# Attention features of a fused kernel: plain f32 in two row tiles, with a new order of steps

## The chip, the cores and the metric

The kernel runs on one core of a Trainium2 chip. The metric is the device time of one execution in microseconds (us); the median of three runs is given. A profile of one further execution shows every instruction of the core's engines: TensorE (PE in the rows, PEld for its weight loads), VectorE (DVE), ScalarE (ACT), GpSimd (POOL), and the queue that issues DMAs (SP).

## The reference

Three stages follow one another. All arrays are float32.

```python
# attention: q, k, v are (2, 8, 576, 64), omega is (128, 64)
def phi(x):                                   # x is q or k, times 64 ** -0.25
    h = x @ omega.T - sum(x * x) / 2          # 128 features of each row
    return exp(h - max(h)) / sqrt(128)
kv, z = phi(k).T @ v, sum(phi(k), rows)
x = (phi(q) @ kv) / (phi(q) @ z + 1e-6)       # -> 1152 tokens x 512
# first MoE block: w_in (512, 2048), w_out (2048, 512)
h = x @ w_in
x = (h * clip(h + 3, 0, 6) / 6) @ w_out
# second one: 8 experts, each token goes to its best one, at most 288 rows per expert
out[i] = gate[i] * relu(x[i] @ w1[e]) @ w2[e]
```

The weights w_in and w_out come as float64. The kernel leaves out `sum(x * x) / 2`, which is the same for all 128 features of a row and cancels against the maximum.

## The kernel before

**Units.** The attention stage works on 18 units, each one load of 256 KB: 128 partitions by four blocks of 128 columns. A block holds two heads' rows on top of each other (64 partitions each), so that a unit has eight groups of 128 rows. Units 0 to 3 are k of the first batch, unit 4 the remainder of k, then q and k alternate, then the rest of q (13 to 17). `seq` lists them. Omega is laid out as a block matrix, 128 partitions by 2 x 128 columns, one omega in the upper half of the rows for the first 128 columns and one in the lower half for the others.

**Steps of a unit**, each with a letter and the unit's number in the plan:

- XH, XL (`halve_x`): x is rounded to float32r on ScalarE (L786), and the rest is subtracted on GpSimd, for units 0 and 1 on VectorE (L788). Omega is split in the same way (L757, L759).
- B (`features`): for each half of the unit six float32r products, three for each of two blocks (L798), into one PSUM bank.
- N: the negative maximum of each row group on VectorE (L804). P: four exponentials of 128 columns on ScalarE, with that maximum as bias (L810).
- for k: K (`kv_acc`), 16 float32 products in two column tiles, 32 records in the trace (L825), accumulated in the pair of banks called acc; KR for the remainder (L836); KW, KV for the sums.
- for q: C (four transposes, L855), T (copy on ScalarE, L859), D (16 products in two column tiles, L871), R, S, X (division on VectorE, L881 to L893), E (four transposes, L899), EH and EL (the result in float32r halves, L922 and L925).

**What comes behind.** H(f, g) is the hidden product of 128 columns of w_in with a third of the tokens, 12 float32r products of 384 columns (L289); 16 x 3 of them follow. The float64 weights are decoded by integer work, mostly on VectorE (L258 to L268), then split (L274, L276; the first four subtractions of w_in on GpSimd). w_out's blocks are transposed (L311) and folded with the gate (L321), for the logits (L346). Then come the routing and two experts (L594 to L711).

**What sets the order.** `Plan` keeps a list of steps with an engine, a cost, the steps that it waits for, buffers taken and freed, and a rank. It plays the steps through and issues each engine's instructions in the order found; an engine then takes them strictly in that order. Among the steps that could start, the lowest rank goes first. Six hidden products (`n < 6`) may stand among the attention's steps, the others wait for all of it.

**Buffers.** PSUM has eight banks: four called tp, two pj, and the pair acc. In SBUF x has 6 buffers (`RAWX`), its halves 3 each (`XB`), phi 3, the maxima 4. All loads are issued by SP, in an order given by `LOADS`; a load of v is 520 KB, of a weight block 512 KB.

Of the kernel before, what the change touches and what calls it, by code (L numbers as in the profile page):

```python
# [136 lines left out]
def moe_kernel(ctx, tc, q, k, v, v_rest, omega, w_in, w_out, w_gate, w1, w2, out, cap):  # L137
    nc = tc.nc
# [25 lines left out]
    RAWX = 6  # L164
    XB = 3
# [3 lines left out]
    IN_TP = {(u, 1) for u in range(5)}  # L169
    X_POOL = set(range(2,18))  # L170
# [13 lines left out]
    DELTA = {'consts': 179.8, 'XH0': 114.8, 'XL0': 28.0, 'OM': 177.0, 'OL': -70.0, 'B0': 22.8, 'N0': 31.9, 'P0': -12.3, 'XH1': -17.1, 'XL1': -201.3, 'B1': -72.7, 'N1': -23.2, 'P1': 171.6, 'XH2': 385.8, 'XL2': -65.0, 'B2': 92.4, 'N2': -38.4, 'P2': 35.8, 'KT': -7.5, 'K0': -121.6, 'KW': 261.7, 'KV': -47.8, 'K1': 249.5, 'C1': 139.8, 'T1': -17.3, 'D1': -25.2, 'R1': 118.8, 'S1': 7.3, 'X1': 130.4, 'E1': 174.3, 'EH1': -25.3, 'EL1': -122.5, 'C2': -83.5, 'T2': -52.0, 'D2': 233.9, 'R2': -10.8, 'S2': 38.3, 'X2': 208.0, 'E2': -40.8, 'EH2': 72.5, 'EL2': -34.9, 'KR': 36.9}  # L184
    RANK = {'A': 0.91, 'B': 1.33, 'C': -3.05, 'D': 2.59, 'E': 3.57, 'EH': 1.06, 'EL': 0.01, 'K': 3.55, 'KV': 3.01, 'N': -2.07, 'P': 2.42, 'R': -1.78, 'T': 3.38, 'XH': -3.59, 'XL': -0.61}
# [564 lines left out]
    wbd = [ap.tile([128, 2, M], F32R, tag=f"wbd{i}", bufs=1, name=f"wbd{i}") for i in range(2)]  # L750
# [40 lines left out]
    def features(u, half):
        hi, lo = xs[u]
        pool, tag = (pt, "tp") if (u, half) in IN_TP else (pp, "pj")
        pj = pool.tile([128, 4, M], F32, tag=tag, name="pj")
        for n, (a, w) in enumerate(((hi, wbd[0]), (hi, wbd[1]), (lo, wbd[0]))):
            for jj in range(2):
                j = 2 * half + jj
                nc.tensor.matmul(  # L798
                    pj[:, 2 * jj:2 * jj + 2, :], lhsT=a[:, j, :], rhs=w,
                    start=(jj == 0 and n == 0), stop=(n == 2), skip_group_check=True,  # L800
                )
        yield
        nm = ap.tile([128, 4], F32, tag="nm", bufs=4, name="nm")
        nc.vector.tensor_reduce(out=nm, in_=pj, axis=AX.X, op=ALU.max, negate=True)  # L804
        yield
# [46 lines left out]
    def turn_phi(u, half):  # L852
# [6 lines left out]
        nc.scalar.activation(out=phTs[u][:, 4 * half:4 * half + 4, :], in_=tp, func=ACTF.Copy)  # L859
# [13 lines left out]
    def attend(u, half):  # L873
# [11 lines left out]
        if b == "R":  # L885
            xo, ni = x.rearrange("p a i d -> p (a i) d")[:, 4 * half:4 * half + 4], nd[:, :, 0:D]
            rr = rd.to_broadcast([128, 4, D])
        else:

            xo = x[:, half:4:2, :, :]  # L890
            ni = nd.rearrange("p (i r) d -> p r i d", r=2)[:, :, :, 0:D]
            rr = rd.rearrange("p (i r) o -> p r i o", r=2).to_broadcast([128, 2, 2, D])
        nc.vector.tensor_tensor(out=xo, in0=ni, in1=rr, op=ALU.mult)  # L893

    def turn_out(u):
# [33 lines left out]
        tp=4, pj=2, acc=1, x=XB, phi=3, phiR=1, phT=2, xo=2, nm=4, rd=4, x32=X32, raww=4, rawx=RAWX, rawv=2,  # L929
# [44 lines left out]
    for u, (nm, b, c, hh) in enumerate(seq):  # L974
        is_r = (nm, b) == ("k", "R")
        gen = halve_x(u)
        parts = parts_of(u)
        for n in range(len(parts)):
            z = "z" * n
            chain(gen, [  # L980
                (f"XH{u}{z}", "ACT", 0.3 if len(parts) == 2 else 0.52, dict(after=[f"Vx{u}{z}"], takes=None if n else "x", rank=rank("XH", u))),
                (f"XL{u}{z}", *(("Pool", 1.23) if u in X_POOL else ("DVE", 0.6 / len(parts))), dict(after=[f"XH{u}{z}"], frees=[f"Lx{u}"], rank=rank("XL", u))),
            ])
            if not u and not n:
                chain(halve_omega(), [
                    ("OM", "ACT", 0.3, dict(after=["Vom"], rank=-20)),
                    ("OL", "DVE", 0.33, dict(after=["OM"], rank=-20)),
                ])
        gens = [features(u, z) for z in range(2)]
        for z in range(2):  # L990
            chain(gens[z], [
                (f"B{z}{u}", "PE", 0.66, dict(after=["XL0z" if z else "XH0", "OL"] if not u else [f"XL{u}"], takes="tp" if (u, z) in IN_TP else "pj", frees=[f"XH{u}"], rank=rank("B", u))),
                (f"N{z}{u}", "DVE", 0.6, dict(after=[f"B{z}{u}"], takes="nm", rank=rank("N", u))),
                (f"P{z}{u}", "ACT", 1.0, dict(
                    after=[f"N{z}{u}"] + [f"P0{u}"] * z, takes=None if z else "phiR" if is_r else "phi",
                    frees=[f"B{z}{u}", f"N{z}{u}"], rank=rank("P", u))),
            ])
# [6 lines left out]
    for b in range(B):  # L1004
        kus = [units["k", b, c, hh] for c in range(2) for hh in range(2)]
        names = []
        for u in kus:
# [4 lines left out]
                name, "PE", 1.2, lambda a=(b, u, c == 0, c == 1): kv_acc(*a),  # L1012
# [420 lines left out]
```

## Time and profile before

| | |
|---|---|
| median of three runs | 314.27 us (313.54 to 314.93) |
| the profiled execution | 314.52 us, its span 312.8 us |
| TensorE busy | 299.8 us, 96% of the span |
| VectorE busy | 219.7 us, 70% |
| ScalarE busy | 176.6 us, 56% |
| GpSimd busy | 59.7 us, 19% |
| granted clock of TensorE | 0.998 on average |

The span goes from the first to the last instruction; what the time has more lies around it. The ends of matmuls are modelled and overlap the next one's start, so the busy time of TensorE is more than the time that it needs. Shares over the whole span mix stages: the attention stage takes about the first quarter, the hidden products and the experts the rest.

### The profile page before, as it was taken

The numbers are of one execution on the slowest core, as the hardware profiler recorded it, in microseconds if no ns is written. First come the engines' busy times: TensorE is split into PE (matmuls) and PEld (weight loads), VectorE is DVE, ScalarE is ACT, GpSimd is POOL, SyncE is SP. The second block draws the span as 40 slices with busy tenths as digits, with TensorE's granted clock in tenths as the row PEclk, the third lists the DMA queues.
The fourth block names the chain that finished last, engine by engine and source line by source line (L and its number), as shares of the span: only waits on it lengthen the run. The fifth ranks groups of instructions, "written<-read, shape, count | busy, mean of one in ns | idle before, by whom it ended". The sixth has DMA issues, their size and how long they took to land.

```text
span 312.8 us, 7069 instructions
## 1 busy us (share of the span) xinstructions
PE 299.8 (96%) x2590; PEld 272.8 (87%) x2590; DVE 219.7 (70%) x492; ACT 176.6 (56%) x426; POOL 59.7 (19%) x73
## 2 busy tenths in 40 slices
PE   8898899999999999999999999999999999999992
PEld 5787788999998989889979888989999889999981
DVE  4469799999999979998899664578936072483300
ACT  5898989995655656456559323636344152543300
POOL 0582435510000000000000000313410170430211
PEclk9999999999999999999999999999999999999999
DMA  7898422472678886899634325986374607702011
GB/s 228 315 344 281 139 70 67 166 258 69 198 248 243 283 284 211 249 262 301 206 127 151 125 53 148 292 266 247 119 253 147 212 34 113 250 2 69 3 44 41
DMA packets 30812, 55.68 MB, mean 178 GB/s; under 512 B 5904, under 2 KB 18576, under 8 KB 30768
## 3 DMA queue, kind: packets, MB, share of 16 engines
q1 hardware_dynamic: 30384, 53.96, 54.0%
q0 software_dynamic: 384, 1.18, 1.0%
q8 instruction: 22, 0.36, 0.5%
q14 instruction: 22, 0.18, 0.2%
HBM read 38.99 MB, written 16.13 MB: 176 GB/s over the span
## 4 chain that ended last, share of the span: by engine, by line
PE 55%; DVE 13%; DMA 11%; issue 9%; ACT 6%; POOL 3%; SPq 1%; POOLq 0%; DVEq 0%; ACTq 0%
PE hp L289 17%; PE yw L594 16%; PE hp L664 7%; DMA raw<-in_w_in_dram 5%; PE pj L798 4%; PE yp L688 4%; ACT phi L810 2%; POOL xl L788 2%; DMA out_dram<-scratch,to 2%; PE lg L346 2%; DVE g L297 2%; DMA raw<-in_w_out_dram 1%; DMA rawx<-in_k_dram 1%; PE tpC L855 1%; DVE nm L804 1%
## 5 line engine op out<-in xcount | busy, mean ns | idle before, releaser
L289 PE MATMUL hp<-xT,wsplit 128*128 128x384 f32 x576 | 108.2, 341 | 0.1
L289 PEld LDWEIGHTS hp<-xT,wsplit 128*128 128x128 f32 x576 | 98.8, 188 | 5.7 <-issue 4.1
L641 POOL TENSOR_TENSOR wsplit<-rawe,wsplit 128x512 fp32r<-128x512 f32 x16 | 23.0, 1457 | 176.7 <-DVE g L297 133.9
L594 PE MATMUL yw<-gh,ohi 128*128 128x288 f32 x256 | 51.8, 297 | 0.4 <-DVE gh L584 0.4
L293 ACT ACTIVATE t<-hp,three 128x384 f32<-128x384 f32 x48 | 27.7, 577 | 28.9 <-PE hp L289 25.2
L810 ACT ACTIVATE phi<-pj,nm 128x128 f32<-128x128 f32 x144 | 40.8, 413 | 3.0 <-DVE nm L804 1.8
L594 PEld LDWEIGHTS yw<-gh,ohi 128*128 128x128 f32 x256 | 41.1, 188 | 1.5 <-DVE gh L584 0.6
L594 PE MATMUL yw<-gh,olo 128*128 128x288 f32 x128 | 37.6, 294 | 0.0
L297 DVE SCALAR_TENSOR_TENSOR g<-t,hp 128x384 f32<-128x384 f32 x48 | 26.3, 547 | 10.3 <-ACT t L293 7.2
L804 DVE TENSOR_REDUCE nm<-pj 128x4 f32<-128x512 f32 x36 | 24.6, 686 | 11.3 <-PE pj L798 10.1
L798 PE MATMUL pj<-wbd,xh 128*128 128x256 f32 x144 | 26.0, 303 | 4.4 <-ACT phi L810 3.4
L798 PEld LDWEIGHTS pj<-wbd,xh 128*128 128x128 f32 x144 | 19.7, 192 | 8.0 <-ACT phi L810 5.4
L788 POOL TENSOR_TENSOR xl<-rawx,xh 128x512 fp32r<-128x512 f32 x16 | 20.9, 1313 | 27.8 <-ACT xh L786 25.1
L664 PE MATMUL hp<-dT,wsplit 128*128 128x288 f32 x192 | 26.0, 296 | 0.0
L584 DVE TENSOR_TENSOR gh<-gw,gh 128x288 fp32r<-128x288 f32 x32 | 16.3, 529 | 13.6 <-ACT gh L582 13.3
L664 PEld LDWEIGHTS hp<-dT,wsplit 128*128 128x128 f32 x192 | 25.7, 188 | 0.0
L582 ACT ACTIVATE gh<-gw 128x288 fp32r<-128x288 f32 x32 | 13.8, 442 | 19.4 <-PE yw L594 15.7
L641 DVE TENSOR_TENSOR wsplit<-rawe,wsplit 128x512 fp32r<-128x512 f32 x16 | 18.1, 1150 | 9.2 <-ACT wsplit L639 9.2
L594 PEld LDWEIGHTS yw<-gh,olo 128*128 128x128 f32 x128 | 24.2, 189 | 0.0
L688 PE MATMUL yp<-wsplit,h 128*128 128x512 f32 x96 | 22.8, 396 | 0.0
L688 PEld LDWEIGHTS yp<-wsplit,h 128*128 128x128 f32 x96 | 17.9, 188 | 4.5 <-issue 0.4
L639 ACT ACTIVATE wsplit<-rawe 128x512 fp32r<-128x512 f32 x32 | 18.5, 621 | 4.3 <-DMA rawe<-in_w_dram 4.3
(150 smaller groups left out, 420.1 us busy)
## 6 DMA issues: line engine op xcount, KB each, us to landing
rawe<-in_w_dram SPq DMA_DIRECT2D x19, 512.0 KB, 5.0
gall<-g SPq DMA_DIRECT2D x48, 192.0 KB, 3.4
raw<-in_w_in_dram SPq DMA_DIRECT2D x16, 512.0 KB, 5.0
raw<-in_w_out_dram SPq DMA_DIRECT2D x16, 512.0 KB, 4.2
gfirst<-g SPq DMA_DIRECT2D x16, 192.0 KB, 2.9
rawx<-in_q_dram SPq DMA_DIRECT2D x9, 256.0 KB, 3.9
out_dram<-blank SPq DMA_DIRECT2D x1, 2304.0 KB, 8.1
gw<-gfirst SPq DMA_DIRECT2D x16, 144.0 KB, 3.5
```

What stands on the lines that cost most here:

```text
L289: nc.tensor.matmul(hp, lhsT=w[:, a, wk], rhs=xT[g][b_][:, kk, :], start=(n == 0), stop=(n == 3 * KD - 1))
L293: nc.scalar.activation(out=t, in_=hp, func=ACTF.Relu, bias=three[:, 0:1])
L297: nc.vector.scalar_tensor_tensor(out=gv, in0=t, scalar=6.0, in1=hp, op0=ALU.min, op1=ALU.mult)
L594: nc.tensor.matmul(self.ps[kk], lhsT=wohalf[f][a][:, kk * 128:(kk + 1) * 128], rhs=self.gh[f][:, b_, :], start=(f == YORDER[0] and n == 0) ...
L639: nc.scalar.activation(out=hi, in_=part, func=ACTF.Copy)
L641: engine.tensor_tensor(out=lo, in0=part, in1=hi.bitcast(F32), op=ALU.subtract)
L664: nc.tensor.matmul(hp, lhsT=self.w[0, f][:, a, kk * 128:(kk + 1) * 128], rhs=self.window.dT[b_][:, kk, :], start=(n == 0), stop=(n == 3 * ...
L688: nc.tensor.matmul(ps_, lhsT=self.h2[f // 4, a][:, f % 4, c * 128:(c + 1) * 128], rhs=self.w[1, f][:, b_, :], start=(n == 0), stop=(n == 3 ...
L788: (nc.gpsimd if u in X_POOL else nc.vector).tensor_tensor(out=lo[:, sl], in0=rawt[u][:, sl], in1=hi[:, sl].bitcast(F32), op=ALU.subtract)
L798: nc.tensor.matmul(pj[:, 2 * jj:2 * jj + 2, :], lhsT=a[:, j, :], rhs=w, start=(jj == 0 and n == 0), stop=(n == 2), skip_group_check=True,)
L804: nc.vector.tensor_reduce(out=nm, in_=pj, axis=AX.X, op=ALU.max, negate=True)
L810: nc.scalar.activation(out=phis[u][:, 4 * half + h, :], in_=pj[:, h, :], func=ACTF.Exp, bias=nm[:, h:h + 1])
```

## The change

- `halve_x` and omega's split are gone. Omega is only scaled, in place, on ScalarE (OM).
- `features` takes x as it was loaded, in float32. For each block there are two products, one on the upper 64 rows and one on the lower, each with 128 columns; the two write different PSUM banks, `pjs[u][0]` and `pjs[u][1]`. A unit has one feature step B0 of eight products.
- `BANKS` names for each unit the pair of banks: two of tp, the two of pj, or acc (units 3, 8, 14, 16, 17), which the sums over k use as well.
- The maximum (N) and the exponentials (P) are steps of their own. For four half units (`LESS`) VectorE adds the negative maximum (Q), and one exponential of 512 columns follows on ScalarE.
- There are nine buffers of x instead of six, five of phi instead of three, six of the maxima; XB is gone.
- The groups of a unit have another numbering (`slot_head`, and the places that read them).
- The ranks of 953 steps are written out by name (`RANKS`), those of the loads on SP too. Among the loads that is x5, x2, x3, x6, x1, x7, x10 (ranks 7.7 to 13.2, behind omega and x0), w0 (16.0), v00 (18.3), x4 (22.6), w2 (23.1), w1 (25.6), v01 (28.0), x12 (33.3), the remainder of v (35.1), and the others from 38.5 up.
- Some planned costs change (K, C, D, E); the order in which the hidden products are listed starts with H(0,0), H(1,0); each hidden product of an expert is planned behind the one before it (`then`).

```diff
-    RAWX = 6
-    XB = 3
+    RAWX = 9
...
-    IN_TP = {(u, 1) for u in range(5)}
-    X_POOL = set(range(2,18))
+    BANKS = "pttapttpattpppapaa"
+    LESS = {(2, 1), (3, 0), (7, 1), (10, 1)}
+    T_DVE = set()
+    PHIB, NMB = 5, 6
+    FIRST, EARLY_H = 2, 6
...
-    wbd = [ap.tile([128, 2, M], F32R, tag=f"wbd{i}", bufs=1, name=f"wbd{i}") for i in range(2)]
...
+    def scale_omega():
+        nc.scalar.activation(out=om, in_=om, func=ACTF.Copy, scale=qscale)
...
-        return (s, 0) if b == "R" else (4 * hh + s // 2, s % 2)
...
+        return (2 * (s % 4) + s // 4, 0) if b == "R" else (4 * hh + s % 4, s // 4)
+
+    pjs, nms = {}, {}
+
+    def features(u):
+        if BANKS[u] == "a":
+            both = pa.tile([128, 8, M], F32, tag="acc", name="pj")
+            pjs[u] = [both[:, 0:4], both[:, 4:8]]
+        else:
+            pool, tag = (pt, "tp") if BANKS[u] == "t" else (pp, "pj")
+            pjs[u] = [pool.tile([128, 4, M], F32, tag=tag, name="pj") for _ in range(2)]
+        for j in range(4):
+            for r in range(2):
+                rows = slice(64 * r, 64 * r + 64)
+                nc.tensor.matmul(pjs[u][r][:, j, :], lhsT=rawt[u][rows, j, :], rhs=om[rows, r, :], start=True, stop=True, skip_group_check=True)
+
+    def feature_max(u, r):
+        if not r:
+            nms[u] = ap.tile([128, 8], F32, tag="nm", bufs=NMB, name="nm")
+        nc.vector.tensor_reduce(out=nms[u][:, 4 * r:4 * r + 4], in_=pjs[u][r], axis=AX.X, op=ALU.max, negate=True)
...
+    def feature_less(u, r):
+        if (u, r) not in LESS:
+            return
+        nc.vector.tensor_tensor(out=phi_of(u, r), in0=pjs[u][r], in1=nms[u][:, 4 * r:4 * r + 4].rearrange("p (h o) -> p h o", o=1).to_broadcast([128, 4, M]), op=ALU.add)
+
+    def feature_exp(u, r):
+        phi = phi_of(u, r)
+        if (u, r) in LESS:
+            nc.scalar.activation(out=phi, in_=phi, func=ACTF.Exp)
+        else:
+            for h in range(4):
+                nc.scalar.activation(out=phi[:, h, :], in_=pjs[u][r][:, h, :], func=ACTF.Exp, bias=nms[u][:, 4 * r + h:4 * r + h + 1])
...
+        plan.add(
+            f"B0{u}", "PE", 1.05, lambda u=u: features(u), after=["OM"] + [f"Vx{u}" + "z" * n for n in range(len(parts_of(u)))],
+            takes=[("acc", f"A{u}")] if BANKS[u] == "a" else [(tag, f"B0{u}"), (tag, f"B1{u}")], frees=[f"Lx{u}"], rank=rank("B", u))
...
-        if st["engine"] in ("PE", "ACT", "DVE", "Pool"):
-            st["rank"] += DELTA.get(st["kind"], 0.0)
+        st["rank"] = RANKS.get(st["name"], st["rank"])
...
-    order = [("H", f, g) for f in range(F1T - TAIL) for g in range(NG)]
+    order = [("H", f, g) for gs in ((0,), range(1, NG)) for f in range(FIRST) for g in gs]
+    order += [("H", f, g) for f in range(FIRST, F1T - TAIL) for g in range(NG)]
```

## Rows read from the trace of the kernel before

**Rows 1.** Windows; per engine: us busy (instructions); then granted clock, DMA share, GB/s.
```profile
0.00:80.00 80.00, 73.86 (x927) 65.58 (x928) 63.86 (x146) 68.12 (x207) 30.33 (x51) 1.00 0.57 194
4.00:20.00 16.00, 14.29 (x184) 12.64 (x185) 8.77 (x14) 13.20 (x44) 8.10 (x26) 1.00 0.95 333
80.00:290.00 210.00, 209.06 (x1527) 193.18 (x1527) 153.63 (x339) 105.28 (x214) 25.22 (x19) 1.00 0.60 188
```

**Rows 2.** Timeline of TensorE: start us, us, instruction, out<-in, count [idle before].
```profile
3.95 1.03 PE L798 MATMUL pj<-wbd,xh 128*128 128x256 f32 x4 [0.38 <-ACT xh L786]
...
79.84 4.41 PE L289 MATMUL hp<-xT,wsplit 128*128 128x384 f32 x24
```

**Rows 3.** Timeline of TensorE in the attention stage, three stretches.
```profile
13.62 0.64 PE L798 MATMUL pj<-wbd,xh 128*128 128x256 f32 x4
14.11 0.40 PE L798 MATMUL pj<-wbd,xl 128*128 128x256 f32 x2
14.35 0.64 PE L798 MATMUL pj<-wbd,xh 128*128 128x256 f32 x4
...
21.33 1.51 PE L836 MATMUL kvr<-restv,phi 128*128 128x130 f32 x12
22.59 0.73 PE L798 MATMUL pj<-wbd,xh 128*128 128x256 f32 x4
...
52.77 0.40 PE L798 MATMUL pj<-wbd,xl 128*128 128x256 f32 x2
53.10 1.15 PE L825 MATMUL kvp<-rawv,phi 128*64 128x65 f32 x32
54.19 0.66 PE L855 MATMUL tpC<-ident,phi 128*128 128x128 f32 x4
54.60 0.72 PE L798 MATMUL pj<-wbd,xh 128*128 128x256 f32 x4
```

**Rows 4.** Lines of TensorE, 0 to 80 us: busy us, mean ns | idle before.
```profile
L798 PE MATMUL pj<-wbd,xh 128*128 128x256 f32 x144 | 26.0, 303 | 4.4 <-ACT phi L810 3.4 <-ACT xh L786 0.8
```

**Rows 5.** Timeline of ScalarE, first and last exponentials.
```profile
5.99 1.14 ACT L810 ACTIVATE phi<-pj,nm 128x128 f32<-128x128 f32 x4
7.44 3.20 ACT L810 ACTIVATE phi<-pj,nm 128x128 f32<-128x128 f32 x12 [0.31 <-DVE nm L804]
10.45 1.75 ACT L786 ACTIVATE xh<-rawx 128x512 fp32r<-128x512 f32 x3
...
71.49 0.60 ACT L859 ACTIVATE phT<-tpC 128x512 f32<-128x512 f32 x1 [0.28 <-PE tpC L855]
71.98 1.13 ACT L810 ACTIVATE phi<-pj,nm 128x128 f32<-128x128 f32 x4
```

**Rows 6.** Lines of ScalarE, 0 to 80 us.
```profile
L810 ACT ACTIVATE phi<-pj,nm 128x128 f32<-128x128 f32 x144 | 40.8, 413 | 3.0 <-DVE nm L804 1.8 <-DVE rd L881 1.1
L786 ACT ACTIVATE xh<-rawx 128x512 fp32r<-128x512 f32 (+1 forms) x19 | 12.2, 663 | 2.7 <-PE pj L798 1.4 <-DMA rawx<-in_k_dram 1.0
```

**Rows 7.** Timelines of VectorE and of GpSimd, about 35 us.
```profile
35.40 1.48 DVE L262 TENSOR_SCALAR x<-x 128x512 f32<-128x512 f32 x1
35.32 1.28 POOL L788 TENSOR_TENSOR xl<-rawx,xh 128x512 fp32r<-128x512 f32 x1 [1.06 <-ACT xh L786]
```

**Rows 8.** Lines of VectorE, 0 to 82 us.
```profile
L804 DVE TENSOR_REDUCE nm<-pj 128x4 f32<-128x512 f32 x36 | 24.6, 686 | 11.3 <-PE pj L798 10.1 <-ACT xh L786 0.7
L266 DVE SCALAR_TENSOR_TENSOR x<-raw,x 128x512 int32<-128x512 int32 x4 | 4.7, 1178 | 0.1
...
L260 DVE TENSOR_SCALAR x<-raw 128x512 int32<-128x512 int32 x4 | 2.3, 566 | 0.7 <-DMA raw<-in_w_in_dram 0.7
...
L266 DVE SCALAR_TENSOR_TENSOR wo<-raw,wo 128x512 int32<-128x512 int32 x2 | 1.4, 688 | 0.0
```

**Rows 9.** Timeline of TensorE at the end of the weights' decode.
```profile
164.92 0.60 PE L311 MATMUL tpW<-ident,wo 128*128 128x128 f32 x4
171.70 1.08 PE L321 MATMUL wogp<-woT,wg 128*32 128x128 f32 x32
```

More of the change, by code (lines that the diff above doesn't have):

```diff
@@ L791, in features @@
[L791 to L805, printed above, removed]
+        return (2 * (s % 4) + s // 4, 0) if b == "R" else (4 * hh + s % 4, s // 4)
@@ L858, in turn_phi @@
             phTs[u] = ap.tile([128, 8, 128], F32, tag="phT", name="phT")
-        nc.scalar.activation(out=phTs[u][:, 4 * half:4 * half + 4, :], in_=tp, func=ACTF.Copy)
+        if (u, half) in T_DVE:
+            nc.vector.tensor_copy(out=phTs[u][:, 4 * half:4 * half + 4, :], in_=tp)
+        else:
+            nc.scalar.activation(out=phTs[u][:, 4 * half:4 * half + 4, :], in_=tp, func=ACTF.Copy)
     nds = {}
@@ L975, in moe_kernel @@
         is_r = (nm, b) == ("k", "R")
[L976 to L997, printed above, removed]
+        if not u:
+            plan.add("OM", "ACT", 0.3, scale_omega, after=["Vom"], rank=-20)
@@ new lines, in moe_kernel @@
+        tag = {"a": "acc", "t": "tp", "p": "pj"}[BANKS[u]]
+        plan.add(
+            f"B0{u}", "PE", 1.05, lambda u=u: features(u), after=["OM"] + [f"Vx{u}" + "z" * n for n in range(len(parts_of(u)))],
+            takes=[("acc", f"A{u}")] if BANKS[u] == "a" else [(tag, f"B0{u}"), (tag, f"B1{u}")], frees=[f"Lx{u}"], rank=rank("B", u))
+        for r in range(2):
+            less = (u, r) in LESS
+            plan.add(f"N{r}{u}", "DVE", 0.6, lambda a=(u, r): feature_max(*a), after=[f"B0{u}"], takes=None if r else "nm", rank=rank("N", u) + 0.1 * r, then=[f"N0{u}"] * r)
+            mine = dict(then=[f"F{u}"] * r, takes=None if r else [("phiR" if is_r else "phi", f"P0{u}")], frees=[f"B{r}{u}", f"A{u}", f"N0{u}"])
+            plan.add(f"Q{r}{u}", *(("DVE", 0.6) if less else ("none", 0.0)), lambda a=(u, r): feature_less(*a), after=[f"N{r}{u}"], rank=rank("Q", u), **(mine if less else {}))
+            plan.add(f"P{r}{u}", "ACT", 0.48 if less else 1.0, lambda a=(u, r): feature_exp(*a), after=[f"{'Q' if less else 'N'}{r}{u}"], rank=rank("P", u) + 0.1 * r, **({} if less else mine))
+            if not r:
+                plan.add(f"F{u}", "none", 0.0, lambda: None, after=[f"{'Q' if less else 'P'}0{u}"])
@@ L1027, in moe_kernel @@
             chain(turn_phi(u, z), [
-                (f"C{z}{u}", "PE", 0.43, dict(after=[f"P{z}{u}"], takes="tp", frees=[f"P0{u}"], rank=rank("C", u), then=[f"D0{qus[x]}" for x in [qus.index(u) - 2] if x >= 0])),
-                (f"T{z}{u}", "ACT", 0.48, dict(
+                (f"C{z}{u}", "PE", 0.41, dict(after=[f"P{z}{u}"], takes="tp", frees=[f"P0{u}"], rank=rank("C", u), then=[f"D0{qus[x]}" for x in [qus.index(u) - 2] if x >= 0])),
+                (f"T{z}{u}", *(("DVE", 0.6) if (u, z) in T_DVE else ("ACT", 0.48)), dict(
                     after=[f"C{z}{u}"] + [f"T0{u}"] * z, takes=None if z else "phT", frees=[f"C{z}{u}"], rank=rank("T", u))),
@@ L1032, in moe_kernel @@
         plan.add(
-            f"D0{u}", "PE", 1.2, lambda u=u: attend_products(u), after=[f"T0{u}", f"T1{u}"] + [f"KV{bb}" for bb in range(B) if b in (bb, "R")],
+            f"D0{u}", "PE", 1.1, lambda u=u: attend_products(u), after=[f"T0{u}", f"T1{u}"] + [f"KV{bb}" for bb in range(B) if b in (bb, "R")],
             takes=[("tp", f"D{z}{u}") for z in range(2)], frees=[f"T0{u}"], rank=rank("D", u))
@@ L1284, in add_expert @@
             chain(x.hidden(f), [
-                (f"h{k}.{f}", "PE", 1.62, dict(after=[f"tl{k}.{kk}" for kk in range(KD)] + [f"v{k}.0{f}"], takes="tp" if f in H_TP else "pj",
+                (f"h{k}.{f}", "PE", 1.62, dict(then=[f"h{k}.{f - 1}"] * (f > 0), after=[f"tl{k}.{kk}" for kk in range(KD)] + [f"v{k}.0{f}"], takes="tp" if f in H_TP else "pj",
                                                frees=[f"u{k}.0{f}", f"d{k}0", f"d{k}1"], rank=r + f)),
@@ L1322, in moe_kernel @@
     ])
+    for st in plan.steps:
+        st["rank"] = RANKS.get(st["name"], st["rank"])
     steps = plan.order()
```

39 lines of the change are left out of this document (14 added, 25 removed).

## The prediction

> **What bounds the kernel now.** I read first the windows, to see where an engine sets the pace. From 80 to 290 us TensorE is busy for 209.06 of 210 us, while VectorE has 153.63 and ScalarE 105.28 [rows 1]: there TensorE alone sets the end, and nothing in the change takes work from that stretch. Whatever the attention stage in front gives back is therefore kept to the end, if the work that feeds the stretch is ready earlier too. Then the timeline of TensorE, for where that stretch begins: the first feature product starts at 3.95 us, and from 79.84 us on the hidden products follow one another [rows 2]. Between them lie 75.9 us.
>
> How much of this is work? Busy times of matmuls overlap, so I take distances from one start to the next [rows 3]. A half unit of features (six products) takes 14.35 - 13.62 = 0.73 us; 32 records of kv products 54.19 - 53.10 = 1.09; four transposes 54.60 - 54.19 = 0.41; twelve records of the remainder's products 22.59 - 21.33 = 1.26, so 0.105 each. By the code, 36 half units make 26.3, 8 kv and 9 attend products 18.5, 16 remainder records 1.7, 18 + 9 groups of transposes 11.1, and three hidden products at about 2.1 make 6.3 us: 63.9 in all. So TensorE stands or waits for some 12.0 us of these 75.9. The listing by line names part of it: 4.4 us ahead of the feature products, mostly for the exponentials, which free their banks [rows 4].
>
> The exponentials are ScalarE's, and its timeline is the tightest there: first group at 5.99 us, last at 71.98, done at about 73.1 [rows 5]. In these 67.1 us it issues everything else around them; the gaps that its lines show are 3.0 us ahead of exponentials and 2.7 us ahead of the rounding of x (L786) [rows 6]. I take ScalarE as the bound of the stage. VectorE is close behind: 63.86 of the first 80 us [rows 1].
>
> **The change, part by part.** *ScalarE.* It loses L786, 16 whole roundings within its stretch (two halves and one more lie ahead of 5.99). Three of them at 10.45 us take 1.75 with the last one's overlap [rows 5]; by the step to the next instruction elsewhere they take 0.52 each, so 8.3 us. Twelve exponentials go from 7.44 to 10.45 us [rows 5], so a half unit is 1.00; for the four half units in LESS one exponential over 512 columns stands in its place, not in the trace, between a transpose copy of the same 512 columns, 71.98 - 71.49 = 0.49 [rows 5], and 1.00. I take 0.52, as it reads SBUF like the rounding: 1.9 us less. Together 10.2 us. The gaps ahead of L786 go with it, save the 1.0 that lies before 5.99: up to 1.7 more, 11.9. If the 3.0 ahead of the exponentials went as well it would be 14.9. The first exponential doesn't move: one feature step, 1.07 (below), and a maximum of 0.69 [rows 8] after x has come at about 4 us give 5.8 against 5.99. I take **11.5 us**, nearer to 11.9, since TensorE and GpSimd stop holding x back.
>
> *TensorE.* 216 float32r products go, 144 float32 products over half the rows come, 16 records for a unit (the remainder's eight products, also float32, show as 16 records [rows 3]). No product over 64 rows is in the trace. The nearest is the remainder's record: 0.105 us for 130 columns, 0.103 for 128, so 16 x 0.103 = 1.65 if the two row tiles don't overlap, 0.83 if they do wholly. For two tiles side by side the kv products are the nearest: by the same rate 32 records of 65 columns would take 1.68 in a row and take 1.09, a factor of 0.65. I take 1.65 x 0.65 = 1.07 for a unit, 19.3 for 18, against 26.3: 7.0 us less, with bounds of 11.4 less and 3.4 more. A bound further out: if each weight load stood in the open, at 0.41 / 4 = 0.10 as in the transposes [rows 3], a unit would take 3.3. Against that end stand the kv records, whose 32 loads hide in 1.09 us. With 11.5 us off and 7.0 less work TensorE still has 12.0 - 4.5 = 7.5 us to wait in, so it fits and doesn't bound.
>
> A rule speaks against this part. From six feature products to a kv product, which works in column tiles, the step is 53.10 - 52.77 = 0.33 us for the last two products, against 14.35 - 14.11 = 0.24 between equal ones [rows 3]: 0.09 for a change of tiling. The Trainium skill, "TensorEngine Tiling (Array Packing)", section Key Properties, says that a change of tiling mode drains TensorE; with 36 more changes at the row's 0.09 the 7.0 us would be 3.8, and without the rule 7.0. The 1.09 already holds such a step, and either leaves ScalarE the bound.
>
> *VectorE.* It loses three subtractions of x and omega's (1.9 us), gains four subtractions of maxima, each like a maximum's 0.69 [rows 8]: +2.8. GpSimd loses 16 subtractions of 1.3 us, and this matters to VectorE: the clamp at 35.40 us takes 1.48 us while one of them runs from 35.32 to 36.60 [rows 7]. The five decode steps of x have four instructions each, from 1178 to 566 ns on average with 688 ns for an undisturbed one of the first kind [rows 8]. Their excess is 4 x 0.49 = 2.0 for the first kind and, by the same subtraction, 6.3 for all; 16 of the 20 long GpSimd instructions go, so about 5.1 come back. Net -4.2: 59.7 us of work, to be done by 68.5 instead of 80. It must stand 8.8 us there, where it stands 16.1 now. That is possible, since features no longer wait for a rounding and a subtraction, but it is the tightest cover here. Behind it lies a lead: the last transpose of w_out starts at 164.92 and the fold that needs it at 171.70 [rows 9], some 6 us by which the decode may lag unseen.
>
> *Queues and buffers.* The loads of x, v and w change places on SP by RANKS; in the first 20 us the DMA engines are 0.95 busy at 333 GB/s [rows 1]. Ahead of v01 stand now omega, nine x and three w and v00, about 4.6 MB or 14 us at that rate; kv of units 2 and 3 waits for it, with units 0 to 3 holding four of five feature buffers until then. ScalarE needs until 5.8 + 7 x 2 = 20 us for the seven units that the buffers take (u4's has its own, u5 and u7 leave theirs after transposes), so this costs nothing; if v01 came after 20 us, it would cost what is over. x's buffer is freed by TensorE now and not by GpSimd, and there are nine. The accumulator's banks serve u3, u8, u14, u16 and u17: kv of the first batch waits for u3's exponentials, behind the same cover. GpSimd's constants move ahead to an idle engine. The slot order, the two more maxima buffers, the hidden products' new order and the `then` of the expert's products move work inside stretches where TensorE is full or waits for others, and I put them at nothing; without that cover they would cost one hidden product, 2.1 us.
>
> **Sum.** The profiled execution took 314.52 us, 0.25 above the median of 314.27. 314.52 - 11.5 = 303.0, or 302.8 beside the median.
>
> **Rivals.**
> *VectorE or the order becomes the bound.* Three engines are then near 88% in a stage of small buffers. If TensorE keeps its 12.0 us of waits it gains its 7.0 alone: 307.5. If VectorE still stands 13 of 80, its 59.7 end at 72.7, 7.3 earlier: 307.2. For it: VectorE stood 11.3 us ahead of its maxima [rows 8]. Against: those features were late because x was rounded and subtracted first.
> *More than the sum.* The exponentials' waits go too: 14.9, 299.6; with the small gaps that no row names, 297.5.
> *Row tiles don't overlap.* 1.65 a unit, 3.4 us more work; TensorE bounds, and with 4.4 us of waits left, as ahead of the feature products now [rows 4], to 8.5 it gains 4 to 0 us; in the middle 12.0 - 3.4 - 6.5 = 2: 312.4. The Trainium skill, "TensorE: Matmul & The Clock Gate", section LDWEIGHTS, has a load cost by its columns and not its rows, 128 / 1.2 = 107 ns; 16 loads one behind the other would then be 1.71 us a unit by that page (an estimate), 30.8 in all and 313.5 for the kernel. No half-height load of 128 columns is in the trace; the nearest, kv's half-width loads, hide.
> *Slower.* The weight loads of the row tiles aren't hidden. Place: the feature step. A unit of c us gives back 12.0 - 7.5 - (18c - 26.3); that is nothing at c = 1.71 and a loss of over 1.6 us from c = 1.80. At 2.0 it is 5.2 lost, 319.7; with every load in the open (3.3) some 343. For it: no such product in the trace. Against: 0.034 us for a load and product of kv.
>
> **How the numbers follow.** My forecast 0.53 (its own range 300.5 to 305.5); VectorE or the order 0.17; more than the sum 0.13; no overlap 0.10; slower 0.07. This kernel's runs lie within 0.5%, 1.6 us, which is what a measurement can tell from no change. Faster are the first three and 0.04 of the fourth: 0.87; the other 0.06 of it the same; slower 0.07. The range takes in the forecast, the second case and most of the third: 297.5 to 309.
>
> **What would show it.** Right: the last exponential at about 60.5 us (71.98 now), hidden products without a break from about 68 us, a unit of features in 1.07 us, no decode step of VectorE over 1 us, ScalarE without gaps over 1 us after 6 us, and TensorE from there to the end as long as now. Wrong: feature steps of 1.6 us or more; VectorE with 13 us or more of idle time in the first 70; a wait for v01 or for u3's banks between 14 and 24 us; gaps on TensorE after 80 us because decoded weights are late.

## The result, and the profile after

The changed kernel took 304.46 us (median; 303.78 to 306.05) against 314.6 us of the kernel before in the same comparison: a ratio of 0.969, 95% interval 0.9645 to 0.9736. Measured again (the first experiment below) it took 303.79 us, ratio 0.966 [0.9626, 0.9695]. The forecast was 302.8.

There are two profiles of it: the first took 306.05 us (span 304.2), the second belongs to the repeat (span 301.8; before 312.8). Windows of the second first, then 4 to 20 us of the first, with the columns of [rows 1]; the last two lines are of the kernel before and answer to the second's 20 to 60 us.

```profile
0.00:80.00 80.00, 77.06 (x1074) 68.67 (x1075) 67.27 (x166) 60.59 (x185) 9.66 (x35) 1.00 0.65 229
4.00:20.00 16.00, 14.57 (x219) 13.05 (x217) 14.06 (x26) 13.62 (x48) 1.23 (x12) 1.00 1.01 386
20.00:40.00 20.00, 19.44 (x399) 17.53 (x396) 18.92 (x48) 17.95 (x60) 3.67 (x3) 1.00 0.67 235
40.00:60.00 20.00, 20.00 (x276) 18.02 (x276) 18.14 (x49) 17.27 (x53) 1.87 (x2) 1.00 0.24 77
80.00:280.00 200.00, 198.52 (x1461) 181.57 (x1460) 140.40 (x320) 101.08 (x206) 24.35 (x19) 1.00 0.57 183
```
```profile
4.00:20.00 16.00, 13.46 (x188) 12.26 (x188) 12.50 (x22) 12.43 (x43) 1.12 (x11) 0.89 1.01 382
```
```profile
20.00:40.00 20.00, 17.78 (x241) 15.93 (x238) 16.35 (x31) 17.71 (x56) 10.07 (x11) 1.00 0.66 222
40.00:60.00 20.00, 19.23 (x266) 17.35 (x264) 18.66 (x46) 19.74 (x63) 8.90 (x8) 1.00 0.19 67
```

The reader is to see a change of place. Between 40 and 60 us ScalarE was busy for 19.74 of 20 us before; now it has 17.27, and TensorE is full. The stage after 80 us, where TensorE stood 0.9 us in 210 before [rows 1], now shows a little more: 1.5 us in 200.

TensorE's timeline in the second profile; it answers to [rows 2], [rows 3] and [rows 9].

```profile
3.50 5.45 PE L792 MATMUL pj<-om,rawx 64*128 64x128 f32 x64
10.03 1.25 PE L792 MATMUL pj<-om,rawx 64*128 64x128 f32 x16 [1.08 <-DMA rawx<-in_q_dram]
...
25.87 0.66 PE L861 MATMUL tpC<-ident,phi 128*128 128x128 f32 x4
26.45 2.08 PE L792 MATMUL pj<-om,rawx 64*128 64x128 f32 x32
...
42.53 1.16 PE L792 MATMUL pj<-om,rawx 64*128 64x128 f32 x16
43.62 0.66 PE L908 MATMUL tpE<-ident,x 128*128 128x128 f32 x4
44.11 0.60 PE L861 MATMUL tpC<-ident,phi 128*128 128x128 f32 x4
44.55 0.60 PE L908 MATMUL tpE<-ident,x 128*128 128x128 f32 x4
...
67.55 4.44 PE L291 MATMUL hp<-xT,wsplit 128*128 128x384 f32 x24
...
155.96 0.66 PE L313 MATMUL tpW<-ident,wo 128*128 128x128 f32 x4
158.63 1.08 PE L323 MATMUL wogp<-woT,wg 128*32 128x128 f32 x32
...
190.18 0.43 PE L596 MATMUL yw<-gh,ohi 128*128 128x288 f32 x2
```

Two more rows of TensorE's timelines, the first from the kernel before, the second from the first profile of the changed one:

```profile
200.53 0.43 PE L594 MATMUL yw<-gh,ohi 128*128 128x288 f32 x2
```
```profile
69.61 4.43 PE L291 MATMUL hp<-xT,wsplit 128*128 128x384 f32 x24
```

A unit of features takes 43.62 - 42.53 = 1.09 us, forecast 1.07. The unbroken hidden products start at 67.55 instead of 79.84, 12.3 us earlier (forecast 11.5). But the first yw product (the gated hidden values times w_out, behind the hidden products) starts at 190.18 instead of 200.53, 10.35 earlier: 1.9 us are lost between. In the first profile the hidden products start at 69.61, 10.2 earlier, after a longer stand of TensorE and a stretch at a lower clock behind it (last section).

ScalarE's timeline in the second profile, answering to [rows 5], and VectorE's lines there from 0 to 72 us, answering to [rows 8].

```profile
6.38 5.26 ACT L816 ACTIVATE phi<-pj,nm 128x128 f32<-128x128 f32 x20 [2.94 <-DVE nm L797]
11.51 0.65 ACT L813 ACTIVATE phi<-phi 128x512 f32<-128x512 f32 x1
12.05 2.18 ACT L816 ACTIVATE phi<-pj,nm 128x128 f32<-128x128 f32 x8
...
42.33 2.17 ACT L816 ACTIVATE phi<-pj,nm 128x128 f32<-128x128 f32 x8 [1.22 <-DVE nm L797]
...
60.02 2.19 ACT L816 ACTIVATE phi<-pj,nm 128x128 f32<-128x128 f32 x8
62.02 0.76 ACT L260 ACTIVATE x<-raw 128x512 f32<-128x512 f32 x1
```
```profile
L797 DVE TENSOR_REDUCE nm<-pj 128x4 f32<-128x512 f32 x36 | 23.2, 683 | 6.3 <-PE pj L792 5.5 <-ACT phi L816 0.8
L268 DVE SCALAR_TENSOR_TENSOR x<-raw,x 128x512 int32<-128x512 int32 x5 | 3.4, 685 | 0.0
L264 DVE TENSOR_SCALAR x<-x 128x512 f32<-128x512 f32 x5 | 2.1, 421 | 0.0
```

The exponentials run from 6.38 to 62.0, 55.6 us instead of 67.1 (forecast 5.8 to 60.5). One over 512 columns takes 12.05 - 11.51 = 0.54 to the next instruction (forecast 0.52). No decode step is stretched any more: 685 ns where [rows 8] has 1178, and GpSimd's busy time from 0 to 80 us is 9.66 instead of 30.33 us. VectorE stands 6.3 us ahead of its maxima, not 11.3, mostly for TensorE.

### The profile page after: what moved, and what is told of

Same layout as the page of the kernel before. It is cut to its first block, busy times and chain, and to the rows that moved or that the text cites. A ratio compares the mean times of both kernels' runs of the same rounds, so it can differ in the third digit from the quotient of the medians.

```text
span 304.2 us, 7089 instructions
## 1 busy us (share of the span) xinstructions
PE 291.6 (96%) x2662; PEld 263.9 (87%) x2662; DVE 209.0 (69%) x492; ACT 164.5 (54%) x395; POOL 37.1 (12%) x57
## 4 chain that ended last, share of the span: by engine, by line
PE 73%; DVE 7%; DMA 6%; ACT 6%; issue 5%; POOL 0%; SPq 0%; POOLq 0%; DVEq 0%; ACTq 0%
PE hp L291 25%; PE yw L596 17%; PE hp L666 7%; DMA raw<-in_w_out_dram 4%; PE pj L792 4%; PE yp L690 4%; ACT phi L816 3%; PE lg L348 3%; PE tpC L861 3%; PE nd L880 2%; DMA out_dram<-scratch,to 2%; PE kvp L831 2%; DVE nm L797 2%; PE tpE L908 1%; PE tpW L313 1%
## 5 line engine op out<-in xcount | busy, mean ns | idle before, releaser
L596 PE MATMUL yw<-gh,ohi 128*128 128x288 f32 x256 | 51.0, 295 | 0.0
L643 POOL TENSOR_TENSOR wsplit<-rawe,wsplit 128x512 fp32r<-128x512 f32 x16 | 21.3, 1344 | 169.7 <-DVE g L299 131.2
L816 ACT ACTIVATE phi<-pj,nm 128x128 f32<-128x128 f32 x128 | 35.7, 436 | 5.9 <-DVE nm L797 5.2
L586 DVE TENSOR_TENSOR gh<-gw,gh 128x288 fp32r<-128x288 f32 x32 | 20.1, 649 | 19.0 <-ACT gh L584 15.5
L797 DVE TENSOR_REDUCE nm<-pj 128x4 f32<-128x512 f32 x36 | 23.2, 683 | 7.8 <-PE pj L792 7.0
L792 PE MATMUL pj<-om,rawx 64*128 64x128 f32 x288 | 21.6, 299 | 2.7 <-ACT phi L816 2.5
L792 PEld LDWEIGHTS pj<-om,rawx 64*128 64x128 f32 x288 | 19.1, 204 | 5.4 <-issue 3.9
L643 DVE TENSOR_TENSOR wsplit<-rawe,wsplit 128x512 fp32r<-128x512 f32 x16 | 12.9, 814 | 7.3 <-ACT wsplit L641 7.2
L676 ACT ACTIVATE h<-hp 128x256 fp32r<-128x256 f32 x16 | 6.1, 384 | 16.4 <-PE hp L666 16.4
```

The source lines that it names most:

```text
L586: nc.vector.tensor_tensor(out=t[:, 1, :], in0=self.raw[f], in1=t[:, 0, :].bitcast(F32), op=ALU.subtract)
L596: nc.tensor.matmul(self.ps[kk], lhsT=wohalf[f][a][:, kk * 128:(kk + 1) * 128], rhs=self.gh[f][:, b_, :], start=(f == YORDER[0] and n == 0) ...
L643: engine.tensor_tensor(out=lo, in0=part, in1=hi.bitcast(F32), op=ALU.subtract)
L792: nc.tensor.matmul(pjs[u][r][:, j, :], lhsT=rawt[u][rows, j, :], rhs=om[rows, r, :], start=True, stop=True, skip_group_check=True)
L797: nc.vector.tensor_reduce(out=nms[u][:, 4 * r:4 * r + 4], in_=pjs[u][r], axis=AX.X, op=ALU.max, negate=True)
L816: nc.scalar.activation(out=phi[:, h, :], in_=pjs[u][r][:, h, :], func=ACTF.Exp, bias=nms[u][:, 4 * r + h:4 * r + h + 1])
```

## The experiments

Theory 1 is the forecast's reason: ScalarE bounds the attention stage, and TensorE has time to spare in it. Theory 2: in the changed kernel TensorE bounds it from about 20 us on. Beside them stand the VectorE rival (GpSimd's traffic on VectorE is a main term) and the rival that the gain is the written order's. All differences below are to the 303.79 us of the repeat, unless it is said otherwise.

**The changed kernel again.**

> The changed kernel once more, unaltered, beside the others of this group. Every theory expects 304.5 us within 0.5%, ratio 0.969 to the kernel before. What is open is the granted clock between 12 and 15.6 us (0.50 in the first profile, after TensorE had stood for 2.5 us) and the 1.2 us gap of TensorE at 129 us: if both belong to the order and not to one execution, they stand in this profile too.

303.79 us (303.13 to 304.29). The profile is the second one above. Neither the fall of the clock (it is 1.00 from 12 to 16 us) nor the gap at 129 us (TensorE runs on from 125.02 to 131.87) came again, so neither stands in every execution of this order.

**The products over the full height.** All 128 rows are multiplied, omega's block matrix having zeros in the half that doesn't belong, so the result is the same; but the two products can't stand side by side:

```diff
-                nc.tensor.matmul(pjs[u][r][:, j, :], lhsT=rawt[u][rows, j, :], rhs=om[rows, r, :], ...)
+                nc.tensor.matmul(pjs[u][r][:, j, :], lhsT=rawt[u][:, j, :], rhs=om[:, r, :], ...)
```

> Each feature product uses all 128 rows, with omega's block matrix (zeros in the other half), so that nothing can overlap: eight products of 128 columns for a unit, about 1.65 us instead of 1.09, 10 us more TensorE work. The order of all instructions stays. Theory 1 (the prediction's): ScalarE sets the pace of the stage and TensorE has some 7.5 us to spare, so 2.5 us more, 307. Theory 2 (from the trace after): from 20 us on TensorE sets the pace, so 8 to 10 us more, 312.5 to 314.5.

313.94 us, ratio 0.9982 [0.9955, 1.0009]: 10.1 us slower than the changed kernel, no different from the kernel before. Windows of it:

```profile
20.00:40.00 20.00, 20.00 (x286) 19.05 (x285) 16.46 (x37) 16.51 (x56) 1.27 (x1) 1.00 0.47 164
40.00:60.00 20.00, 20.00 (x328) 19.15 (x327) 15.94 (x46) 14.86 (x46) 2.51 (x2) 1.00 0.21 68
```
```profile
48.03 1.95 PE L792 MATMUL pj<-om,rawx 128*128 128x128 f32 x16
49.91 0.28 PE L880 MATMUL nd<-kvz,phT 128*64 128x65 f32 x2
```
```profile
DVE nm L797 <- PE pj L792: 14.1, 12, 5.7
```

The second fence is TensorE's timeline, the third VectorE's waits up to 75 us (in total, times, longest): a unit now takes 49.91 - 48.03 = 1.88 us, 0.79 more than in row tiles, 14.2 for 18 units. TensorE is busy without a gap, and VectorE stands 14.1 us ahead of its maxima for features. The reduced work of ScalarE and GpSimd, the buffers and the order are all still there, and with TensorE's features at full height they give nothing. (That is a little more than taking TensorE's saving back: features now take 35.3 us, before 31.5, as the table below shows.) The 14.2 us of work cost 10.1, as theory 2 expected, and not 2.5.

To see where TensorE's time goes I added the distances from one group's start to the next by kind, from the first feature product to the unbroken hidden products; in brackets the part that the trace shows as idle ahead of the next group (my sums over the timelines; the ends of matmuls are modelled, so short waits can hide in the rest):

| us | before | changed (second profile) | full height |
|---|---|---|---|
| features | 31.5 (0.8) | 22.3 (1.1) | 35.3 (0.4) |
| kv and attend | 21.7 (1.6) | 18.3 (0.3) | 18.1 |
| the remainder of v | 1.7 | 2.4 | 1.9 |
| transposes | 14.4 (2.2) | 14.3 (0.4) | 13.0 |
| three hidden products | 6.5 | 6.8 | 6.7 |
| together | 75.9 (4.6) | 64.1 (1.7) | 75.0 (0.4) |

**More work on ScalarE.** One copy of 512 columns that nobody reads, ahead of the exponentials of each unit's first half, so 18:

```diff
+        if r == 0:
+            nc.scalar.activation(out=idle_out, in_=idle_in, func=ACTF.Copy)
```

> ScalarE copies 512 columns of a constant once for each unit, in front of its exponentials, nobody reads the copy: about 18 x 0.52 = 9.4 us of the work that the rounding of x was, without its waits. Theory 1 (ScalarE sets the pace): 8 to 9 us more, 312.5 to 313.5. Theory 2 (TensorE sets it from 20 us on, ScalarE only before): the nine units with exponentials before 25 us cost 4 to 5 us, the others 1 to 2: 309 to 311.

309.95 us, ratio 0.9859 [0.9814, 0.9903]: 6.2 slower for 18 copies, 9.4 us by the 0.52 to the next instruction. So ScalarE has about 3 us to spare in the stage, not nine and not none. It may be somewhat more: in this profile the granted clock was 0.89 from 4 to 20 us, as in the first profile of the changed kernel, and 2.1 of the 6.2 us were lost by the second kv product (20.02 instead of 17.88), a part of them to the clock. A window shows ScalarE full again, and TensorE standing:

```profile
20.00:40.00 20.00, 17.54 (x333) 15.46 (x332) 16.11 (x40) 19.95 (x63) 2.25 (x2) 1.00 0.64 222
```

**More work on GpSimd, twice.** First a subtraction that reads the unit's features, 16 of them, then one that reads a constant and the maxima, so that no feature buffer waits for it:

```diff
+        if r == 1 and u > 1:
+            nc.gpsimd.tensor_tensor(out=idle_out, in0=phis[u][:, 0:4]..., in1=phis[u][:, 4:8]..., op=ALU.subtract)
```
```diff
+        if r and u > 1:
+            nc.gpsimd.tensor_tensor(out=idle_out, in0=idle_in, in1=nms[u][:, 0:1].to_broadcast([128, 512]), op=ALU.subtract)
```

> GpSimd subtracts 512 columns for each of units 2 to 17 when their exponentials are done, nobody reads the result: the 16 subtractions of 1.3 us are back on the shared way to SBUF, but on nobody's path. The prediction put their price at 5.1 us of VectorE time. Theory 1 and 2 (VectorE is not the bound): 0 to 1.5 us more, 304.5 to 306. Rival (VectorE sets the pace): 4 to 5 us more, 308.5 to 309.5.

> The GpSimd load of before once more, but its subtraction reads a constant and the unit's maxima, so that it holds no feature buffer and starts with the maxima. If the 7 us were the shared way to SBUF, 309 to 311 again. If they came from the held feature buffers, 304 to 305.5.

The first took 311.16 us, ratio 0.9875 [0.9818, 0.9932], the second 304.86, ratio 0.9685 [0.9647, 0.9723]. A window and lines of the first, then lines of the second, the lines for 0 to 72 us:

```profile
20.00:40.00 20.00, 16.52 (x278) 14.73 (x279) 19.48 (x40) 15.61 (x54) 12.21 (x15) 0.91 0.51 177
L819 POOL TENSOR_TENSOR idle_out<-phi 128x512 fp32r<-128x512 f32 x16 | 21.7, 1357 | 36.0 <-ACT phi L817 35.6 <-ACT phi L814 0.3
L266 DVE TENSOR_SCALAR x<-x 128x512 int32<-128x512 int32 x5 | 5.2, 1044 | 0.1
```
```profile
L802 POOL TENSOR_TENSOR idle_out<-idle_in,nm 128x512 fp32r<-128x512 f32 x16 | 17.0, 1061 | 25.0 <-DVE nm L800 20.6 <-DVE rd L895 4.2
L266 DVE TENSOR_SCALAR x<-x 128x512 int32<-128x512 int32 x5 | 2.1, 425 | 0.1
L264 DVE TENSOR_SCALAR x<-x 128x512 f32<-128x512 f32 x5 | 2.8, 563 | 0.0
```

The 7.4 us of the first looked like the traffic on VectorE (1044 ns for 426): between 20 and 40 us VectorE is busy for 19.48 of 20 us (18.92 in the repeat), TensorE stands for 3.03 us ahead of 32.78, and its granted clock is 0.91 on average. The second loads GpSimd for 17 us and costs 1.1, less than the spread of its runs. It doesn't fully acquit the traffic: its instruction reads one tensor and a column, and stretches VectorE's steps less. What it shows is that 17 us of GpSimd work beside the stage need not cost more than about 1 us. How the first's 7.4 us divide between held buffers, stretched steps and the clock stays open.

**The default order.** The written ranks are dropped, and no unit uses the accumulator's banks; every operation is the same:

```diff
-    BANKS = "pttapttpattpppapaa"
+    BANKS = "ptptptptptptptptpt"
-    RANKS = {"Lx1": 12.0546, ...}
+    RANKS = {}
```

> The new features without the written order: RANKS is empty, so every step has the rank that its stage and unit give it, and the units take pj and tp in turn, none the accumulator's banks. The work is the same on each engine. Theory 2 (TensorE's work and its waits in the first 20 us set the gain): the work taken from TensorE and ScalarE stays taken, 306 to 309. Rival (the gain is the order's; three engines near their limit need one that is fitted to their times): 311 or more, no faster than the kernel before.

322.5 us, ratio 1.0269 [1.0224, 1.0314]: slower than before, by 18.7 us behind the changed kernel. TensorE's timeline in it, then ScalarE's:

```profile
61.95 0.60 PE L861 MATMUL tpC<-ident,phi 128*128 128x128 f32 x4
68.80 3.73 PE L880 MATMUL nd<-kvz,phT 128*64 128x65 f32 x64 [6.24 <-ACT phT L868]
```
```profile
67.05 0.66 ACT L260 ACTIVATE x<-raw 128x512 f32<-128x512 f32 x1 [7.97 <-DMA raw<-in_w_in_dram]
```

The longest stand of TensorE, 6.24 us, is named after the copy of transposes on ScalarE. But ScalarE, which takes its instructions in the planned order, stood itself for 7.97 us with the first decode step of a weight block whose load had not landed, and the copy was behind that step. So here an early place in the order made an engine that others needed wait for a DMA. Behind the stand TensorE's granted clock was 0.50 from 68 to 72 us. These are 6.24 of the 18.7 us; the rest was not taken apart.

**Buffers or order.** Six buffers of x, as before, make the planner write another order; so there are four corners, and three of them were run beside the repeat. In the first both are six, in the second the planner counts six and memory has nine, in the third the planner counts nine and memory has six:

```diff
-    RAWX = 9
+    RAWX = 6
```
```diff
-    RAWX = 9
+    RAWX = 6
...
-        t = rawt[u] = ap.tile([128, 4, 128], F32, tag="rawx", bufs=RAWX, name="rawx")
+        t = rawt[u] = ap.tile([128, 4, 128], F32, tag="rawx", bufs=9, name="rawx")
```
```diff
-        t = rawt[u] = ap.tile([128, 4, 128], F32, tag="rawx", bufs=RAWX, name="rawx")
+        t = rawt[u] = ap.tile([128, 4, 128], F32, tag="rawx", bufs=6, name="rawx")
```

> Six buffers of x, as before the change, instead of nine; the planner moves some steps for it. Theory 2: x is there early enough either way, 303.8 to 305. Rival (the early loads of nine units are part of the gain): 306 or more.

> The planner still works with six x buffers, so that every engine gets the order of the six-buffer kernel (118 and some places of TensorE's list differ from the changed kernel), but the memory has nine. Theory A, the six-buffer kernel lost its 14.3 us by its order (TensorE waits for late VectorE steps behind the new places): 316 to 319, as with six. Theory B, it lost them because its x loads wait for a free buffer and hold SP's queue: 303 to 307, as the changed kernel. Between 308 and 314: both.

> The other corner: the order of the changed kernel on every engine, with six x buffers in memory, so that a load of x can start only when the products of the unit six places earlier have read theirs. Theory A (order alone): 303 to 306, since with x loaded in SP's order TensorE seldom needs a unit's x within six units of its load. Theory B (buffers): 312 to 319, the loads of weights behind a waiting x load come later and VectorE with them. If both corners are near 304 only the two together cost.

| | six buffers | nine buffers |
|---|---|---|
| order for nine | 303.53, ratio 0.9644 [0.9616, 0.9673] | 303.79, ratio 0.966 [0.9626, 0.9695] |
| order for six | 318.12, ratio 1.0124 [1.0084, 1.0164] | 317.98, ratio 1.0099 [1.0055, 1.0142] |

With either order the buffers are worth nothing; the order is worth 14 us. Windows of the second corner (order for six, nine buffers) and TensorE's waits in it from 56 to 200 us (in total, times, longest):

```profile
60.00:80.00 20.00, 16.28 (x179) 13.81 (x174) 16.52 (x48) 8.63 (x22) 0.90 (x2) 0.83 0.65 221
80.00:200.00 120.00, 113.53 (x795) 100.68 (x795) 90.95 (x192) 62.95 (x120) 0.00 (x0) 1.00 0.54 182
```
```profile
PE hp L291 <- DVE g L299: 3.7, 3, 2.5
PE tpE L908 <- DVE x L902: 2.2, 2, 1.7
```

In a worse order TensorE stands for VectorE, at the end of the attention stage (x of the attended rows) and again among the hidden products. A part of the 14 us is its clock, 0.83 on average from 60 to 80 us.

**VectorE behind the attention stage.** To price the 1.9 us lost there, the clamp step of the decode is left out for the 24 late weight blocks (10 us of VectorE; these weights are then not clamped):

```diff
-        nc.vector.tensor_scalar(out=xf, in0=xf, scalar1=HI_CLAMP, scalar2=LO_CLAMP, op0=ALU.min, op1=ALU.max)
+        if key not in abs_act:
+            nc.vector.tensor_scalar(out=xf, in0=xf, scalar1=HI_CLAMP, scalar2=LO_CLAMP, op0=ALU.min, op1=ALU.max)
```

> The clamp of the decode (one of its five steps) is left out for the 24 weight blocks whose sign step is on ScalarE: 24 x 0.42 = 10 us less VectorE work, nearly all of it after the attention stage; the order stays. Theory 2: behind 67.5 us the changed kernel loses about 2 us against the one before, because decoded weights and the products' second steps come late on VectorE: 1.5 to 2 us less, 302. Rival (that loss is in the loads or the queue on SP): no change, 303.8 within 0.5.

301.27 us, ratio 0.9586 [0.9558, 0.9613], 2.5 faster. Two rows of its TensorE timeline:

```profile
67.15 4.43 PE L292 MATMUL hp<-xT,wsplit 128*128 128x384 f32 x24
187.82 0.43 PE L597 MATMUL yw<-gh,ohi 128*128 128x288 f32 x2
```

From the one to the other are 120.67 us; in the kernel before 200.53 - 79.84 = 120.69, in the changed one 190.18 - 67.55 = 122.63. So the 1.9 us are VectorE's late decode, and without it they return.

**The clamp on GpSimd.** A version that keeps the clamp and gives it to the idle engine, for all 24 late blocks and for every second one:

```diff
-        nc.vector.tensor_scalar(out=xf, in0=xf, ...)
+        (nc.gpsimd if key in abs_act else nc.vector).tensor_scalar(out=xf, in0=xf, ...)
```
```diff
+        (nc.gpsimd if key in abs_act and key[1] % 2 else nc.vector).tensor_scalar(out=xf, in0=xf, ...)
```

> A version that might beat the changed kernel: the clamp step of the 24 late weight blocks goes from VectorE to GpSimd, which is idle between 66 and 190 us. VectorE loses 24 x 0.42 = 10.2 us. Theory 2 (after 68 us it is VectorE's late steps that stop TensorE, worth the 2.5 us that leaving the step out gave): 301 to 303. Rival: on GpSimd the step takes about 1.3 us (its subtraction of 512 columns takes 1.31), so every block is ready 0.9 us later, and VectorE's own steps run slower beside it (as 1044 ns for 425 in the run with GpSimd subtractions): 304 to 308.

> The same for every second of the late blocks: VectorE loses 5.1 us. Theory 2: 302 to 303.5. Rival (later blocks, slower VectorE): 303.5 to 306, half of what the run with all 24 shows.

302.92 us, ratio 0.9637 [0.9575, 0.9699], and 304.43, ratio 0.9683 [0.9648, 0.9717]. Neither can be told from the changed kernel. In the first's profile the yw products start at 188.48, 1.7 earlier, so some of it may be there; the interval doesn't say. A clamp of GpSimd takes 674 to 740 ns, not the 1.3 us that was feared.

## Why the prediction was right in its time and wrong in its reason

**What held.** The price of a unit of features by the overlap of the kv products (1.09 for 1.07); the exponential of 512 columns (0.54 for 0.52); the stretch of the exponentials, 11.5 us shorter (55.6 for 67.1); hidden products from about 68 us (67.55); decode steps without stretching; no stand for v01. The time, 304.46 and 303.79, lies in the likeliest case's own range. Two signs of being right failed: ScalarE has gaps over 1 us (1.22 ahead of 42.33), and TensorE takes longer behind the stage than before (below).

**The step that failed** is "TensorE still has 12.0 - 4.5 = 7.5 us to wait in, so it fits and doesn't bound". The 12.0 were what was left of 75.9 us after each kind had been priced by one undisturbed step, 63.9 us together. Most of that isn't waiting that more work could fill: the trace shows 4.6 us of it as idle before, and 1.7 in the changed kernel, 1.3 of these ahead of 20 us. The other 7.4 are TensorE's own steps, dearer than those that the forecast took. Before, these are the features above all: 30.7 us without the idle part, priced at 26.3; then kv and attend (20.1 for 18.5) and transposes (12.2 for 11.1). A half unit ahead of a kv product, for one, takes 53.10 [rows 3] - 52.19 = 0.91 us, not 0.73:

```profile
52.19 0.74 PE L798 MATMUL pj<-wbd,xh 128*128 128x256 f32 x4
```

In the changed kernel TensorE's steps take 62.4 us without the idle part, where the forecast had 56.9 and 7.5 to wait in. Here the transposes are the largest part (13.9 for 11.1): four of them, priced at 0.41, take 26.45 - 25.87 = 0.58 next to products in tiles and 44.55 - 44.11 = 0.44 next to one another. Short waits may hide in these sums, but the full-height run decides that the rest is no room. It put in 14.2 us: the features' distances grew by 13.0 (of the missing 1.2, 0.7 is their idle part, 1.1 down to 0.4), 2.1 came back, mostly as transposes and the remainder, which got shorter, and the stage grew by 10.9, the kernel by 10.1. The rival "row tiles don't overlap" gave 312.4 for this and is what that run built: 313.94.

The Trainium skill, "TensorEngine Tiling (Array Packing)", section Key Properties, says that a change of tiling mode drains TensorE. The 0.58 against 0.44 agrees with it. At full height, where the features work in no row tiles, transposes take 13.0 instead of 13.9 us without the idle parts and the remainder 1.9 instead of 2.4. That is 1.4 us, less than half of the 3.2 by which the forecast's two branches (7.0 and 3.8 us saved) differ. Against the kernel before, kv and attend products got 2.1 us shorter, and TensorE's steps without the idle parts 8.9 (71.3 to 62.4), more than either branch has.

**Why the time came out all the same.** ScalarE's loss of work (16 roundings at 0.52 and four times 1.00 - 0.54, 10.2 us as in the forecast) and TensorE's (8.9 us) are nearly equal. The forecast didn't know the second as a bound, so that its time came out right is luck in this. Before, ScalarE set the pace and TensorE was close behind, as the rows read; no run loaded the kernel before to show it. Now TensorE does, with ScalarE some 3 us behind. ScalarE's loss of work without TensorE's gives nothing, as the full-height run shows, with 3.8 us more of features than before. TensorE's without ScalarE's was not tried as such; the run with the copies comes near it, since it gives 9.4 of the 10.2 us back to ScalarE, and it keeps 4.4 of the 10.5 us (309.95 against 314.34 of the kernel before beside it). So neither loss alone gives the gain.

**GpSimd's contention**, worth 5.1 us of VectorE in the forecast, went as forecast in the steps' durations; that it set the time is not borne out by the second GpSimd run, and the first leaves it open.

**Put at nothing, half rightly:** "The slot order, the two more maxima buffers, the hidden products' new order" and the rest of that sentence, "I put them at nothing; without that cover they would cost one hidden product, 2.1 us". The three more buffers of x are worth nothing. The order of the steps is a condition of the whole gain: the same operations in two other orders cost 14 and 19 us more, not 2.1. The cover was there only in the order that was written.

**The lead behind the stage.** "Some 6 us by which the decode may lag unseen": the lead from the last transpose of w_out to its fold is now 158.63 - 155.96 = 2.7 us, and VectorE's lateness costs 1.9 us in total, as the run without the clamp shows. The forecast named this among the signs of being wrong and gave it no term. The sum of the second profile is so 12.3 us in front, less 1.9 behind, and 0.6 by which the part from the first yw product to the end is shorter (111.6 instead of 112.3): 11.0, its span against that of before (301.8, 312.8), where the forecast had 11.5. A gain of 0.8 us over the forecast in front and a loss of 1.3 behind so cancel in part, which is luck too.

## What to carry to other kernels

Before calling an engine's leftover time "room", look at what the trace names as idle; a stage's length less its steps at their best also holds all that they take beyond that (7.4 of 12.0 us here), and that is no room for more work. Where two engines are both near full, an edit pays only as far as the second allows, so ask of every edit which engine is next, and price its steps as they stand in the trace on average, not at their best. And a hand-written order is part of the change's cost: the same operations, planned differently, went from 3.4% faster to 1.0% and 2.7% slower.

## What the runs showed of the hardware

- Two row tiles of 64 rows in plain float32 overlap: 1.09 us for a unit's eight products, 1.88 at full height, a factor of 0.58 and not 0.5.
- The clock fell after a stand. In the first profile TensorE stood 2.54 us for the exponentials ahead of 10.99 and took up work again; between 12 and 13 us its granted clock went to half speed (0.50, the lower of its two levels, 1.2 and 2.4 GHz), where it stayed until about 16 us; windows and timeline of it:

```profile
12.00:13.00 1.00, 1.00 (x10) 0.88 (x7) 0.84 (x2) 1.00 (x5) 0.00 (x0) 0.73 1.02 386
13.00:15.00 2.00, 2.00 (x15) 1.67 (x15) 1.97 (x5) 2.00 (x8) 0.00 (x0) 0.50 1.04 422
16.00:17.00 1.00, 1.00 (x33) 0.93 (x32) 1.00 (x2) 0.26 (x1) 0.00 (x0) 1.00 1.01 402
```
```profile
10.99 1.25 PE L792 MATMUL pj<-om,rawx 64*128 64x128 f32 x16 [2.54 <-ACT phi L816]
13.84 2.08 PE L792 MATMUL pj<-om,rawx 64*128 64x128 f32 x16
15.85 1.15 PE L831 MATMUL kvp<-rawv,phi 128*64 128x65 f32 x32
```

The unit that starts at 13.84 takes 2.01 us to the next start, where an undisturbed one at full clock takes 1.09 and the same one in the repeat 1.64 (12.24 to 13.88). In the repeat TensorE stood 1.08 us at the same place, and the clock stayed at 1.00. Of the 2.1 us by which the hidden products start later in the first profile, about 1.0 are the longer stand (10.99 for 10.03) and about 1.0 the slower clock behind it (4.86 us from there to the kv product, for 3.85).
- GpSimd's clamp of 512 columns takes 674 to 740 ns, its subtraction 1357, and beside the second a VectorE step of the decode went from 426 to 1044 ns on average, beside the first the w_in blocks' step went from 425 to 471, that of w_out's stayed (424, 422).
